# Banded attention with a two-layer network: the first block's second layer in another order of its tiles, with other landing times in the table that orders the work

## The chip, the cores and the metric

The kernel runs on one core of one Trainium2 chip. A core has five engines that each work through a list of instructions in order: PE (TensorE, matmuls into the PSUM banks), DVE (VectorE), ACT (ScalarE), POOL (GpSimd) and SP (SyncE). DMA transfers are issued from the lists of ACT, SP and POOL and are carried by 16 DMA engines. A transfer is recorded by a semaphore when it lands. The metric is the device time of one execution, in microseconds (us). Engines wait for each other through semaphores, and an instruction that waits holds everything behind it in its engine's list, DMA issues included.

## The reference

Attention over 8 batches, 8 heads, 576 positions and head size 64, in which a query sees itself and the 63 positions before it; then a two-layer network with a leaky activation over all 4608 tokens.

```python
scores = scale * np.matmul(q, k.transpose(0, 1, 3, 2))
mask = (rel >= 0) & (rel < window)                 # window = 64
attn = softmax(np.where(mask, scores, -1e9))
x = np.matmul(attn, v).transpose(0, 2, 1, 3).reshape(B * S, H * D)      # 4608 x 512
h = x @ w_in                                       # w_in 512 x 2048
g = np.maximum(0.01 * h, h)
return g @ w_out                                   # w_out 2048 x 512
```

The results are float32. The kernel gets that accuracy from matmuls on a shorter type by splitting each operand into a high and a low part and multiplying three times (high by high, high by low, low by high).

## The kernel before

**Stages.** The first three chunks of 512 tokens are done the plain way, while the weights are still unpacked. The other six chunks form three blocks (s = 0, 1, 2) of 1024 tokens, that is two half-tiles of 512 tokens, t = 0 and t = 1. The first layer of a block (line 1117, tiles `m{s}_{f}_{k}`) takes seven products instead of eight for each f of 0 to 7 (a Strassen scheme on sums of x and of w_in). The second layer of blocks 1 and 2 also goes in seven products (line 1180, tiles `z`), and needs sums of w_out; the second layer of block 0 goes the plain way (line 1137, tiles `y`): this is the loop at the end of the function, and I call it the y stage. In the trace it runs from about 427 to 544 us.

**The y stage.** Each half-tile t needs 16 row blocks f of g, taken in pairs. A pair p of column half j (f = 8j + 2p and the next) is 1024 wide. ACT makes its high part (`wide_high`, line 1162), DVE its low part (`wide_low`, line 1166), PE then does 24 matmuls into four PSUM banks, one bank for each 128 rows of the output. High and low parts have two buffers that take turns (`gs` and `pxa`). At the end of a half-tile the four banks are copied out (`put_out`, line 1140; banks 0 and 2 by DVE, 1 and 3 by ACT) and sent to `outT`. The next half-tile, and after it block 1, begins with bank 0 again, so these two places are seams: PE can't go on before the bank is copied.

**What stands beside it.** While the blocks run, attention goes on in units m of 128 tokens (two 64-position windows): scores on PE (line 278), a mask on DVE (666), a copy on ACT (672), the maximum over partitions on POOL (681), a subtraction on DVE (688), exp on ACT (692), the sum on POOL (684), five transfers on SP that gather and spread the sums (two at 695, one at 716, two at 728), the values on PE (740), a product on DVE (752), and a transfer to `x_rows` (755). Units 20 to 27 become the x of block 1 (`x_build`: a fetch at 867, sums on DVE at 874, casts on ACT at 893 and DVE at 896). The eight sums of w_out (`prepare(1, f)`) pass one after the other through one buffer, `pspare`: two fetches from `w_second` (1027, issued by ACT), an addition and four smaller ones on DVE (1032, 1035), a cast on ACT (1038), a subtraction on DVE (1041), and two transfers to `w_sums` (1045, issued by ACT). The next sum's fetch may not start before both have landed. Loads of q and k for a unit (170) and of v (174) are issued by ACT as well. The weights for PE are fetched by POOL (1101).

**What sets the order.** Nothing is ordered by hand here. Every step is entered as an `op` with an engine, a duration `us`, the steps that it needs, a `rank` (the smaller goes first), a `lag` after those steps, and `land`, the time that a transfer is taken to need. `arrange()` plays these numbers through and writes each engine's list; it also counts eight lanes, so that a transfer of ACT or SP is not placed before the one eight transfers earlier has landed by its numbers. On the chip the same eight lanes are semaphores: an issue waits until the earlier transfer on its lane has really landed. `bulk` enters ACT's transfers, `load` those of SP. A number of the table never changes what is computed, only where an instruction stands.

Of the kernel before, what the change touches and what calls it, by code (L numbers as in the profile page):

```python
# [86 lines left out]
IN_PREP_AT = (0, 0, 0, 6, 7, 0, 6, 7)  # L87
OUT_PREP = 1.0
IN_SEVEN = (1, 2)
KT = DM // P  # L90
FT = DF // P
# [13 lines left out]
def band_attention_ffn(ctx: ExitStack, tc: tile.TileContext, qk, vW, vL, w_in, w_out, eye_mask, out, outT):  # L105
# [433 lines left out]

    def bulk(fn, *after, rank=1.0, land=6.5):  # L540
        return op("ACT", 0.5, fn, *after, rank=rank, lag=1.0, land=land)

# [228 lines left out]
    def attend(m, gate):  # L771
# [4 lines left out]
        if m > PAIRED + 1:  # L776
            o["k"] = bulk(partial(load_qk, m), before["S"], rank=0.2 + late)
        elif m > PAIRED:
            o["k"] = bulk(partial(load_k, m, nc.scalar), before["S"], rank=0.2 + late)
        if m > PAIRED:  # L780
            o["v"] = bulk(partial(load_v, m, nc.scalar), before["X1"], rank=0.3 + late)
        takes = [before["take"], two["take"]] if m == EARLY else []
# [69 lines left out]
    def x_build(s, n, xt_of, xt_free, x_free):  # L852

        urge, wait = ((0.2, 0.2), (1.4, 2.6), (0.6, 2.6))[s]
        m = (UPC * LEAD + 2 * UPC * s) // UNITS + 2 * n

        def raw():
            return xt_of()[0].rearrange("p (i q c) -> p i q c", i=2, q=4)

        def sums():  # L860
            return xt_of()[1].rearrange("p (k i c) -> p k i c", k=4, i=2)

        def part(q):
            return raw()[:, :, q] if q < 4 else sums()[:, q - 4]

        def fetch():
            nc.sync.dma_start(
                xt_of()[0].rearrange("p (i c) -> p i c", i=2), x_rows[m : m + 2].rearrange("i p c -> p i c")
            )

        got = [load(fetch, *at[m]["kept"], *at[m + 1]["kept"], *xt_free, rank=urge, land=6.5)]

        def sub(to, a, b):
            nc.vector.tensor_tensor(part(to), part(a), part(b), ALU.subtract)

        d = op("DVE", 0.5, partial(sub, 4, 0, 2), *got, rank=urge, lag=wait)
        d3 = op("DVE", 0.5, partial(sub, 6, 1, 0), *got, rank=urge, lag=wait)
        d2 = op("DVE", 0.5, partial(sub, 5, 1, 4), d, rank=urge)
        d4 = op("DVE", 0.5, partial(sub, 7, 3, 5), d2, rank=urge)
# [12 lines left out]
        for a, b, after in ((0, 2, got), (2, 3, got), (3, 7, [d, d2, d3, d4])):  # L892
            hi = op("ACT", 0.2 + 0.213 * (b - a), lambda a=a, b=b: nc.scalar.copy(x_view(0, a, b), source(a, b)), *after, *x_free, rank=urge, lag=wait)
# [4 lines left out]
            done.append(op("DVE", 0.2 + 0.35 * (b - a), low, hi, rank=urge))  # L898
        return done
# [112 lines left out]
    def prepare(n, f, at, hurry, *freed):  # L1012
# [38 lines left out]
        written = [y for x in (f, f + half) for y in stores[x]] if n else []  # L1051
        got = [bulk(partial(fetch, i), *freed, *all_in, *written, rank=hurry + 0.1, land=6.5) for i in range(2)]
        if n:
# [6 lines left out]
        lo = op("DVE", 1.4, low, hi, rank=hurry)  # L1060
        prepared[n, f] = [bulk(partial(keep, i), lo, rank=hurry + 0.1, land=6.5) for i in range(2)]

# [140 lines left out]
    def second_in_seven(s):  # L1203
        WIDE, HIGH = 1.27, 1.07
        last_pair = at[NU // 2 - 1]
# [6 lines left out]
        for k, (slot, t, j) in enumerate(FACTORS):  # L1212
            b = bank_at(s, BANK_OF[k])
            for p in range(4):
# [20 lines left out]
                if p % 2 == 0:  # L1235
                    made_before = [y for f in range(half) for y in prepared[1, f]] if isinstance(slot, int) else []
                    q, got = filled(factor(slot, 2 * p), *made_before)
# [49 lines left out]
    for s in range(NS):  # L1287
# [42 lines left out]
        for t in range(2):  # L1330
            for f in range(FT):
                if f % 2 == 0:
                    q = next(pair_of)
                    j, p = f // half, f % half // 2
                    free = pair_free.get(q % 2, []) + (shut if q % 2 else [])
                    hi = op("ACT", 1.07, partial(wide_high, s, 2 * (q % 2), t, j, p), made[t, f], made[t, f + 1], *free, rank=0.2)
                    lo = op("DVE", 1.6, partial(wide_low, s, 2 * (q % 2), t, j, p), hi, rank=0.2)
                    split_of[t, f] = split_of[t, f + 1] = lo
                g_free[t, f] = [split_of[t, f]]
                if f % 2 == 0:  # L1340
                    n, got = filled(w_second[:, f : f + 2])
# [85 lines left out]
```

## Time and profile before

| what | value |
|---|---|
| three runs | 865.08, 867.63, 868.66 us (median 867.63) |
| profiled execution, its own time | 867.03 us |
| span of its records | 865.2 us |
| PE busy | 848.2 us, 98% |
| DVE, ACT, POOL busy | 72%, 44%, 43% |
| DMA from HBM and to it | 172.52 MB and 53.06 MB |
| y stage in the trace | about 427 to 544 us |

PE is busy nearly all the time, so the time of the kernel is PE's work plus the few places where PE stands still or runs at a lower clock. What ends a standstill is read in the view of waits and then in the timeline of the engine that is named there.

### The profile page before, as it was taken

Reading aid. Unit: us, or ns where it says so; the run is one execution under the profiler, and the core shown is the slowest. Engines: PE = TensorE matmul, PEld = TensorE weight load, DVE = VectorE, ACT = ScalarE, POOL = GpSimd, SP = SyncE. Lnnn points to the kernel's source line nnn. Section 1 sums busy time; section 2 is a strip of 40 time slices with the busy share of each in tenths; the row PEclk is TensorE's granted clock in tenths of the full one; section 3 lists DMA queues with packets and bytes.
Section 4 is the critical chain, followed back from the end, with each engine's and each line's share of the span. In section 5 each row is a group of like instructions: output and inputs, shape, how many; then the busy total and the mean of one; then the engine's idle time right before and its main releaser. Section 6 shows DMA issues by size and latency. Waiting matters only on the chain.

```text
span 865.2 us, 16790 instructions
## 1 busy us (share of the span) xinstructions
PE 848.2 (98%) x6778; PEld 688.3 (80%) x6778; DVE 623.6 (72%) x883; ACT 376.8 (44%) x605; POOL 368.0 (43%) x218
## 2 busy tenths in 40 slices
PE   9999999999999999999999899899999999999998
PEld 6787888888888888888887687688888888888886
DVE  7999885667788778665677879396579865536863
ACT  4665554334334353543533533244354433334431
POOL 5322000878888524667785757655110100011010
PEclk9999999999999999999999999899999999999999
DMA  9874856798899878899989997979987876666672
GB/s 328 259 247 132 267 170 239 249 299 274 295 315 331 274 241 281 299 314 355 305 291 351 306 367 238 373 233 331 284 236 228 235 245 221 193 183 189 204 210 92
DMA packets 99341, 226.80 MB, mean 262 GB/s; under 512 B 15552, under 2 KB 46400, under 8 KB 89792
## 3 DMA queue, kind: packets, MB, share of 16 engines
q0 software_dynamic: 23136, 90.18, 33.2%
q10 hardware_dynamic: 35664, 77.31, 27.0%
q1 hardware_dynamic: 40464, 58.24, 20.2%
q8 instruction: 53, 0.87, 0.4%
q14 instruction: 24, 0.20, 0.1%
HBM read 172.52 MB, written 53.06 MB: 261 GB/s over the span
## 4 chain that ended last, share of the span: by engine, by line
PE 81%; DMA 7%; DVE 6%; issue 2%; POOL 2%; ACT 1%; ACTq 0%; SPq 0%; POOLq 0%; DVEq 0%
PE m L1117 26%; PE z L1180 18%; PE acc L928 10%; PE h L919 10%; PE h L431 5%; PE acc L467 4%; PE s L278 3%; DMA rows<-late_c 3%; PE o L740 3%; DMA late_r<-rows 2%; POOL late_o L684 1%; DMA w_sums<-pspare 1%; DMA raw<-w_out 1%; PE o L367 1%; DVE pspare L1035 1%
## 5 line engine op out<-in xcount | busy, mean ns | idle before, releaser
L1117 PE MATMUL m<-pfew,p 128*128 128x512 f32 x720 | 170.7, 393 | 0.0
L1117 PEld LDWEIGHTS m<-pfew,p 128*128 128x128 f32 x720 | 135.5, 189 | 28.7
L928 PE MATMUL acc<-p,gs 128*128 128x512 f32 x324 | 80.6, 394 | 0.0
L1126 DVE TENSOR_TENSOR p<-m,pxa 128x512 f32<-128x512 f32 x60 | 41.4, 690 | 50.8 <-PE m L1117 50.5
L1101 POOL DMA_DIRECT2D p<-w_first x42 | 22.7, 541 | 124.4 <-PE m L1117 76.7
L1117 PE MATMUL m<-pxb,p 128*128 128x512 f32 x288 | 71.7, 396 | 3.7 <-ACT p L1129 3.7
L681 POOL PARTITION_ALL_REDUCE g<-late_f x20 | 38.7, 1966 | 83.8 <-DVE late_f L666 71.3
L684 POOL PARTITION_ALL_REDUCE late_o<-late_f x20 | 65.2, 3272 | 15.4 <-ACT late_f L692 8.6
L1129 ACT ACTIVATE p<-p 128x512 f32<-128x512 f32 x60 | 37.8, 631 | 76.7 <-DVE p L1126 71.8
L928 PEld LDWEIGHTS acc<-p,gs 128*128 128x128 f32 x324 | 59.8, 188 | 12.8
L1126 DVE TENSOR_TENSOR pxa<-m,pxa 128x512 f32<-128x512 f32 x60 | 41.3, 689 | 36.6 <-PE m L1117 35.8
L1117 PEld LDWEIGHTS m<-pxb,p 128*128 128x128 f32 x288 | 54.5, 191 | 15.6 <-ACT p L1129 4.1
L684 POOL PARTITION_ALL_REDUCE late_o<-e x18 | 59.9, 3347 | 13.2 <-ACT e L692 8.5
L684 POOL PARTITION_ALL_REDUCE late_o<-late_e x18 | 59.8, 3345 | 5.7 <-ACT late_e L692 5.4
L1180 PE MATMUL z<-gs,p 128*128 128x512 f32 x240 | 57.7, 389 | 0.0
L919 PE MATMUL h<-pxa,p 128*128 128x512 f32 x228 | 54.9, 390 | 0.0
L1180 PEld LDWEIGHTS z<-gs,p 128*128 128x128 f32 x240 | 45.1, 188 | 9.3
L1180 PE MATMUL z<-third,p 128*128 128x512 f32 x216 | 51.9, 389 | 0.0
L1180 PE MATMUL z<-pxa,p 128*128 128x512 f32 x216 | 51.9, 389 | 0.0
L1137 PE MATMUL y<-gs,p 128*128 128x512 f32 x192 | 47.4, 399 | 4.3 <-ACT pxa L1162 2.8
L919 PEld LDWEIGHTS h<-pxa,p 128*128 128x128 f32 x228 | 42.7, 188 | 9.0
L1137 PE MATMUL y<-pxa,p 128*128 128x512 f32 x192 | 47.3, 395 | 1.8 <-DVE pxa L1166 1.8
(191 smaller groups left out, 1715.8 us busy)
## 6 DMA issues: line engine op xcount, KB each, us to landing
p<-w_first POOLq DMA_DIRECT2D x42, 1024.0 KB, 6.1
p<-w_second POOLq DMA_DIRECT2D x28, 1024.0 KB, 6.7
p<-w_sums POOLq DMA_DIRECT2D x16, 1024.0 KB, 5.5
qk<-qk ACTq DMA_DIRECT2D x26, 512.0 KB, 6.0
pspare<-w_second ACTq DMA_DIRECT2D x16, 512.0 KB, 7.0
w_sums<-pspare ACTq DMA_DIRECT2D x16, 512.0 KB, 8.3
raw<-w_out ACTq DMA_DIRECT2D x15, 512.0 KB, 4.0
raw<-w_in ACTq DMA_DIRECT2D x14, 512.0 KB, 3.9
```

The source lines that it names most:

```text
L278: nc.tensor.matmul(ps[j][t, c : c + QB], k[i][s, p], q[s, w, p], start=not begun and (not more or (w, p) == (0, 0)), stop=not begun and no ...
L431: nc.tensor.matmul(ps, a[:, k, :], b[:, k, part], start=n == 0, stop=n == len(terms) - 1)
L467: nc.tensor.matmul(acc[c, i], a[:, ts], b, start=begin and n == 0, stop=end and n == 2)
L681: nc.gpsimd.partition_all_reduce(most_of(j), e_of(m)[:, j], P, ReduceOp.max)
L684: nc.gpsimd.partition_all_reduce(sum_of(j), e_of(m)[:, j], P, ReduceOp.add)
L919: nc.tensor.matmul(ps, a[:, k, :], b[:, k], start=i == 0, stop=i == len(terms) - 1)
L928: nc.tensor.matmul(acc[c, i], a[:, i * P : (i + 1) * P], b, start=begin and k == 0, stop=n in ends and k == 2)
L1117: nc.tensor.matmul(tiles[b], w[:, 256 * i + 128 * kt : 256 * i + 128 * kt + 128], x_part(OF_X[k], j, kt), start=begin and c == 0, stop=c = ...
L1126: nc.vector.tensor_tensor(to(), tiles[b], x(), ALU.add)
L1129: nc.scalar.activation(to(), to() if b is None else tiles[b], AF.Prelu, alpha=0.01)
L1137: nc.tensor.matmul(tiles[i], a, b, start=f == 0 and k == 0, stop=f == FT - 1 and k == 2)
L1180: nc.tensor.matmul(tiles[b + i], a, x, start=begin and f == 0 and c == 0, stop=f == half - 1 and c == 2, skip_group_check=not begin,)
```

## The change

In the y stage the pairs are taken tile by tile of g: for each p both column halves, (p, j = 0) and (p, j = 1), then the next p; before, all four p of the first half came first. A tile of g holds both halves of a pair, so it is done with after two neighbouring pairs. The four output rows of a half-tile are now staged in the tile of p = 3. The pair's high part is entered ahead of its weights' fetch, as before; only the position in the loop changes. The rest of the diff changes numbers of the table: the rank of the w_out sums (1.0 to 0.6), longer landings and lags for the loads of q, k and v of the units from 20 on, for the fetches and stores of the w_out sums and for the fetches of x, some durations, and the w_sums fetch for four f waits for those four sums instead of all eight.

```diff
-OUT_PREP = 1.0
+OUT_PREP = 0.6
-    def bulk(fn, *after, rank=1.0, land=6.5):
-        return op("ACT", 0.5, fn, *after, rank=rank, lag=1.0, land=land)
+    def bulk(fn, *after, rank=1.0, lag=1.0, land=6.5):
+        return op("ACT", 0.5, fn, *after, rank=rank, lag=lag, land=land)
-            o["k"] = bulk(partial(load_qk, m), before["S"], rank=0.2 + late)
+            o["k"] = bulk(partial(load_qk, m), before["S"], rank=0.2 + late, lag=1.0 + 2 * late, land=6.5 + 2 * late)
...
-            o["v"] = bulk(partial(load_v, m, nc.scalar), before["X1"], rank=0.3 + late)
+            o["v"] = bulk(partial(load_v, m, nc.scalar), before["X1"], rank=0.3 + late, lag=1.0 + 2 * late, land=6.5 + 2 * late)
...
-        got = [load(fetch, *at[m]["kept"], *at[m + 1]["kept"], *xt_free, rank=urge, land=6.5)]
+        got = [load(fetch, *at[m]["kept"], *at[m + 1]["kept"], *xt_free, rank=urge, land=8.0 if s else 6.5)]
...
-        got = [bulk(partial(fetch, i), *freed, *all_in, *written, rank=hurry + 0.1, land=6.5) for i in range(2)]
+        got = [bulk(partial(fetch, i), *freed, *all_in, *written, rank=hurry + 0.1, lag=1.0 + 2 * n, land=6.5 + 1.5 * n) for i in range(2)]
...
-        prepared[n, f] = [bulk(partial(keep, i), lo, rank=hurry + 0.1, land=6.5) for i in range(2)]
+        prepared[n, f] = [bulk(partial(keep, i), lo, rank=hurry + 0.1, land=6.5 + 3 * n) for i in range(2)]
...
-                    made_before = [y for f in range(half) for y in prepared[1, f]] if isinstance(slot, int) else []
+                    made_before = [y for f in range(2 * p, 2 * p + 4) for y in prepared[1, f]] if isinstance(slot, int) else []
...
-            for f in range(FT):
+            for f in (j * half + 2 * p + a for p in range(4) for j in range(2) for a in range(2)):
...
-                        where = t, 12 + i
+                        where = t, (6, 7, 14, 15)[i]
```

`late` is 0.45 for the units from 20 on and 0 before, so their loads of q, k and v go from lag 1.0 and landing 6.5 to 1.9 and 7.4. With n = 1 (the w_out sums) the fetches go from lag 1.0 and landing 6.5 to 3.0 and 8.0, and the stores from 6.5 to 9.5. The numbers of SP's small transfers stay. The durations entered for DVE's work on x in block 2 go from 0.5 to 0.42 a step, and those of the wide casts by a few hundredths. In the changed program the lines from 855 on are numbered one higher.

The first place is DVE's list at the seam between the half-tiles. `y_0_0` and `y_0_2` are banks 0 and 2 of half-tile 0, `pspare` is the buffer of a w_out sum, `gs` and `pxa` the low parts of a pair. Before:

```order
L688 TENSOR_TENSOR late_f<-s_0_4978,g 128x512
L1166 TENSOR_TENSOR gs_82<-p_33_3673,gs_81 128x1024
L688 TENSOR_TENSOR late_f<-s_1_4979,g 128x512
L1032 TENSOR_TENSOR pspare_1786<-pspare_1786 128x1024
L1140 COPY p_25_3089<-y_0_0_4619 128x512
L1140 COPY p_24_2972<-y_0_2_4631 128x512
```

With the change:

```order
L688 TENSOR_TENSOR late_f<-s_0_4997,g 128x512
L1167 TENSOR_TENSOR gs_82<-p_33_3674,gs_81 128x1024
L688 TENSOR_TENSOR late_f<-s_1_4998,g 128x512
L1141 COPY p_24_2972<-y_0_0_4620 128x512
L1141 COPY p_24_2972<-y_0_2_4636 128x512
```

The wide addition of a w_out sum no longer stands ahead of the copy of bank 0; it now comes two pairs later.

The second place is ACT's list at the seam between block 0 and block 1. `y_1_1` and `y_1_3` are banks 1 and 3 of half-tile 1, `m_0_0` is the first bank of block 1, which the second product group of block 1 needs again. Before:

```order
L1140 COPY p_26_3246<-y_1_1_5114 128x512
L672 COPY e<-s_0_5599 128x512
L672 COPY e<-s_1_5600 128x512
L1140 COPY p_23_2922<-y_1_3_5167 128x512
L170 DMA qk_83<-qk 128x1024
L1123 COPY pxa_39_5678<-m_0_0_5659 128x512
L1027 DMA pspare_1786<-w_second 128x2x512
L692 ACTIVATE e<-e 128x512
L1027 DMA pspare_1786<-w_second 128x2x512
L692 ACTIVATE e<-e 128x512
L1129 ACTIVATE p_33_3673<-p_33_3673 128x512
L1129 ACTIVATE p_36_3803<-m_0_0_5659 128x512
```

With the change:

```order
L1046 DMA w_sums<-pspare_1786 512x1x256
L1141 COPY p_23_2922<-y_1_1_5118 128x512
L1046 DMA w_sums<-pspare_1786 512x1x256
L692 ACTIVATE late_f<-late_f 128x512
L1141 COPY p_23_2922<-y_1_3_5135 128x512
L699 ACTIVATE late_c_1772<-late_c_1772 128x8
L1124 COPY pxa_39_5615<-m_0_0_5592 128x512
L692 ACTIVATE late_f<-late_f 128x512
L1130 ACTIVATE p_33_3674<-p_33_3674 128x512
L672 COPY e<-s_0_5638 128x512
L1130 ACTIVATE p_36_3805<-m_0_0_5592 128x512
L170 DMA qk_83<-qk 128x1024
```

The two halves of the next sum's fetch and the load of q and k stood ahead of the activation that frees the first bank of block 1 (the last row, `m_0_0` into `p_36`). With the change that activation stands ahead of the load of q and k, and the fetch comes nine rows behind the rows shown. One of a sum's two stores now stands between the copies of banks 1 and 3; before, both stood directly ahead of these rows.

The third place is ACT's list within the y stage, from the stores of one sum to the fetch of the next. `pxb` and `pfew` are casts of x for block 1. Before:

```order
L1045 DMA w_sums<-pspare_1786 512x1x256 x2
L672 COPY late_e<-s_0_4827 128x512
L170 DMA qk_84<-qk 128x1024
L672 COPY late_e<-s_1_4828 128x512
L692 ACTIVATE late_e<-late_e 128x512
L893 CAST pxb_3413<-p_36_3803 128x2x256
L1162 CAST gs_81<-p_25_3089 128x1024
L692 ACTIVATE late_e<-late_e 128x512
L174 DMA more_v<-vL 128x1024
L699 ACTIVATE late_c_1772<-late_c_1772 128x8
L893 CAST pfew_3422<-p_36_3803 128x256
L1027 DMA pspare_1786<-w_second 128x2x512 x2
```

With the change:

```order
L1046 DMA w_sums<-pspare_1786 512x1x256 x2
L894 CAST pfew_3420<-p_37_4012 128x256
L699 ACTIVATE late_c_1772<-late_c_1772 128x8
L1163 CAST gs_81<-p_24_2972 128x1024
L692 ACTIVATE late_e<-late_e 128x512 x2
L174 DMA more_v<-vL 128x1024
L1163 CAST pxa_38_4632<-p_24_2972 128x1024
L894 CAST pfew_3420<-p_37_4012 128x4x256
L672 COPY late_f<-s_0_4997 128x512
L672 COPY late_f<-s_1_4998 128x512
L170 DMA qk_83<-qk 128x1024
L1028 DMA pspare_1786<-w_second 128x2x512
```

Between the stores and the fetch one wide cast (1162) stood before, two stand now (1163). The load of q and k stood between two score copies; now it and the fetch stand directly ahead of a wide cast, which is the next row behind those shown. At two further places of the y stage the load of q and k stands now with only a sum's cast (1039) between it and a wide cast.

More of the change, by code (lines that the diff above doesn't have):

```diff
@@ L776, in attend @@
         if m > PAIRED + 1:
-            o["k"] = bulk(partial(load_qk, m), before["S"], rank=0.2 + late)
+            o["k"] = bulk(partial(load_qk, m), before["S"], rank=0.2 + late, lag=1.0 + 2 * late, land=6.5 + 2 * late)
         elif m > PAIRED:
-            o["k"] = bulk(partial(load_k, m, nc.scalar), before["S"], rank=0.2 + late)
+            o["k"] = bulk(partial(load_k, m, nc.scalar), before["S"], rank=0.2 + late, lag=1.0 + 2 * late, land=6.5 + 2 * late)
         if m > PAIRED:
-            o["v"] = bulk(partial(load_v, m, nc.scalar), before["X1"], rank=0.3 + late)
+            o["v"] = bulk(partial(load_v, m, nc.scalar), before["X1"], rank=0.3 + late, lag=1.0 + 2 * late, land=6.5 + 2 * late)
         takes = [before["take"], two["take"]] if m == EARLY else []
@@ L852, in x_build @@
     def x_build(s, n, xt_of, xt_free, x_free):
+        STEP, WIDTH = (0.42, 0.27) if s == 2 else (0.5, 0.35)
         urge, wait = ((0.2, 0.2), (1.4, 2.6), (0.6, 2.6))[s]
@@ L869, in fetch @@
             )
-        got = [load(fetch, *at[m]["kept"], *at[m + 1]["kept"], *xt_free, rank=urge, land=6.5)]
+        got = [load(fetch, *at[m]["kept"], *at[m + 1]["kept"], *xt_free, rank=urge, land=8.0 if s else 6.5)]
         def sub(to, a, b):
             nc.vector.tensor_tensor(part(to), part(a), part(b), ALU.subtract)
[L876 to L879, printed above, removed]
+        d = op("DVE", STEP, partial(sub, 4, 0, 2), *got, rank=urge, lag=wait)
+        d3 = op("DVE", STEP, partial(sub, 6, 1, 0), *got, rank=urge, lag=wait)
+        d2 = op("DVE", STEP, partial(sub, 5, 1, 4), d, rank=urge)
+        d4 = op("DVE", STEP, partial(sub, 7, 3, 5), d2, rank=urge)
         def x_view(i, a, b):
@@ L896, in low @@
                 nc.vector.tensor_tensor(x_view(1, a, b), source(a, b), x_view(0, a, b).bitcast(F32), ALU.subtract)
-            done.append(op("DVE", 0.2 + 0.35 * (b - a), low, hi, rank=urge))
+            done.append(op("DVE", STEP - 0.27 + WIDTH * (b - a), low, hi, rank=urge))
         return done
@@ L1203, in second_in_seven @@
     def second_in_seven(s):
-        WIDE, HIGH = 1.27, 1.07
+        WIDE, HIGH = 1.22, 1.06
         last_pair = at[NU // 2 - 1]
@@ L1335, in band_attention_ffn @@
                     free = pair_free.get(q % 2, []) + (shut if q % 2 else [])
-                    hi = op("ACT", 1.07, partial(wide_high, s, 2 * (q % 2), t, j, p), made[t, f], made[t, f + 1], *free, rank=0.2)
+                    hi = op("ACT", 1.06, partial(wide_high, s, 2 * (q % 2), t, j, p), made[t, f], made[t, f + 1], *free, rank=0.2)
                     lo = op("DVE", 1.6, partial(wide_low, s, 2 * (q % 2), t, j, p), hi, rank=0.2)
                     split_of[t, f] = split_of[t, f + 1] = lo
+                    n, got = filled(w_second[:, f : f + 2])
                 g_free[t, f] = [split_of[t, f]]
-                if f % 2 == 0:
-                    n, got = filled(w_second[:, f : f + 2])
                 for i in range(4):
```

## The prediction

> **What bounds the kernel now.** I read the head of the page first, then PE's waits.
>
> ```profile
> span 865.2 us, 16790 instructions
> PE 848.2 (98%) x6778; PEld 688.3 (80%) x6778; DVE 623.6 (72%) x883; ACT 376.8 (44%) x605; POOL 368.0 (43%) x218
> ```
>
> ```profile
> PE m L1117 <- ACT p L1129: 3.7, 1, 3.7
> PE y L1137 <- ACT pxa L1162: 2.8, 1, 2.8
> PE y L1137 <- DVE pxa L1166: 1.8, 2, 1.0
> PE y L1137 <- DVE gs L1166: 1.5, 1, 1.5
> ```
>
> PE's work sets the end, and the change takes none of it away. What can be won is PE's standstills. These five waits hold 9.8 us, and all lie in the y stage or just behind it; the list's other waits are smaller and lie in the first 70 us, where nothing changes. The windows of 10 us add that a long standstill costs more than itself (after the times: busy time of PE, PEld, DVE, ACT and POOL, then the granted clock):
>
> ```profile
> 460.00:470.00 10.00, 8.52 (x37) 6.74 (x38) 5.22 (x8) 4.04 (x8) 6.70 (x4) 1.00 1.01 357
> 480.00:490.00 10.00, 7.22 (x71) 5.33 (x72) 9.40 (x11) 5.14 (x9) 8.61 (x4) 0.86 1.01 325
> 550.00:560.00 10.00, 6.35 (x22) 4.86 (x21) 1.58 (x3) 3.43 (x8) 6.35 (x3) 0.77 1.06 376
> ```
>
> The wait of 1.5 left the clock at 1.00; those of 2.8 and 3.7 brought it to 0.86 and 0.77. Undisturbed, PE's pace is in the chain of waits, where 336 matmuls in a row take 76.16, that is 0.227 each, or 5.44 for a pair of 24:
>
> ```profile
> 632.96 76.16 PE z L1180 x336
> ```
>
> What the slow clock costs is in PE's timeline (start, duration, count; what counts is the distance from one start to the next):
>
> ```profile
> 470.76 0.27 PE L278 MATMUL s<-qk,qk 64*64 64x64 f32 x2
> 471.86 4.42 PE L1137 MATMUL y<-gs,p 128*128 128x512 f32 x18
> ...
> 485.80 3.01 PE L1137 MATMUL y<-gs,p 128*128 128x512 f32 x9 [2.78 <-ACT pxa L1162]
> 488.75 0.37 PE L278 MATMUL s<-qk,qk 64*64 64x64 f32 x2
> ...
> 490.65 3.03 PE L1137 MATMUL y<-gs,p 128*128 128x512 f32 x12
> ...
> 557.00 2.93 PE L1117 MATMUL m<-pxb,p 128*128 128x512 f32 x6 [3.65 <-ACT p L1129]
> 559.73 4.08 PE L1117 MATMUL m<-pfew,p 128*128 128x512 f32 x12
> 563.74 0.27 PE L278 MATMUL s<-qk,qk 64*64 64x64 f32 x2
> ```
>
> A unit's scores take 471.86 - 470.76 = 1.10 undisturbed. After the 2.78, nine matmuls took 2.95 (2.04 is due) and the scores 1.90: 1.71 lost. After the 3.65, six took 2.73 (1.36 due) and twelve 4.01 (2.72 due): 2.66 lost. So the seam between the half-tiles costs 2.78 + 1.71 = 4.49, the seam to block 1 costs 3.65 + 2.66 = 6.31, and the three waits within the stage 1.5 + 1.8 = 3.3 by the list above: **14.1 us in all**, the most that there is to win.
>
> The Trainium skill (TensorE: Matmul & The Clock Gate, Part 1, "What's actually happening") has the clock halved only after an idle window of about 3.4 us, in a window that runs freely. By that rule the 2.78 would have cost nothing beyond itself, and the gain below would be 1.7 smaller. The rows contradict it for this stall, and the sum goes by the rows.
>
> Next, why PE waited. ACT's timeline (ACTq rows are DMA issues):
>
> ```profile
> 462.15 0.33 ACTq L170 DMA_DIRECT2D qk<-qk  x1
> 462.58 0.59 ACT L672 COPY late_e<-s 128x512 f32<-128x512 f32 x1 [5.10 <-DMA rows<-late_c]
> 464.11 1.05 ACT L1162 CAST gs<-p 128x1024 fp32r<-128x1024 f32 x1
> ...
> 512.35 1.05 ACT L893 CAST pfew<-p 128x1024 fp32r<-128x1024 f32 x1 [4.66 <-DMA w_sums<-pspare]
> ...
> 545.45 0.59 ACT L1123 COPY pxa<-m 128x512 f32<-128x512 f32 x1 [1.02 <-PE m L1117]
> 552.21 0.57 ACTq L1027 DMA_DIRECT2D pspare<-w_second  x1
> 554.70 0.57 ACTq L1027 DMA_DIRECT2D pspare<-w_second  x1
> 556.37 0.58 ACT L1129 ACTIVATE p<-m 128x512 f32<-128x512 f32 x1
> ```
>
> ACT did nothing from 546.0 to 552.2, because the next row of its list was a fetch for a sum whose buffer was still being stored; the activation that frees block 1's first bank stood behind both halves of that fetch, and PE resumed as it ended (556.95). The waits of 5.10 and 4.66 are of the same kind: a load of q and k held until an earlier transfer on its lane had landed, and the second half of a sum's fetch, both with wide casts behind them. The waits of 1.5 and 0.8 within the stage follow these two; the one of 1.0 follows a low part that DVE began late. The landings in 440 to 560 us say why (median us from issue to landing last):
>
> ```profile
> w_sums<-pspare ACTq DMA_DIRECT2D x6, 512.0 KB, 11.7
> qk<-qk ACTq DMA_DIRECT2D x7, 512.0 KB, 8.0
> p<-x_rows SPq DMA_DIRECT2D x4, 512.0 KB, 9.6
> rows<-late_c SPq DMA_DIRECT2D x8, 4.0 KB, 6.7
> ```
>
> The table counted on 6.5 for the first three and 5.0 for the last. The seam between the half-tiles is another matter, for which DVE's and POOL's timelines are needed:
>
> ```profile
> 468.14 1.21 DVE L1166 TENSOR_TENSOR gs<-p,gs 128x1024 fp32r<-128x1024 f32 x1
> ...
> 481.84 0.68 DVE L688 TENSOR_TENSOR late_f<-s,g 128x512 f32<-128x512 f32 x1
> 482.44 2.66 DVE L1032 TENSOR_TENSOR pspare<-pspare 128x1024 f32<-128x1024 f32 x1
> 485.02 1.27 DVE L1140 COPY p<-y 128x512 f32<-128x512 f32 x2
> ...
> 528.93 1.21 DVE L1032 TENSOR_TENSOR pspare<-pspare 128x1024 f32<-128x1024 f32 x1
> ```
>
> ```profile
> 481.49 3.52 POOL L684 PARTITION_ALL_REDUCE late_o<-late_f  x1
> ```
>
> The view of waits names ACT, but its cast had ended by 485.1. Bank 0 was copied by DVE from 485.02 (half of 1.27 for the first of two), and PE went on at 485.80. Ahead of that copy stood the wide addition of a w_out sum, which took 2.66 beside a POOL sum and 1.21 without one.
>
> **The change part by part.** The sum is made against the profiled execution's own 867.03 (span 865.2); the median of the runs, 867.63, is 0.60 above it.
>
> *Fetch and q, k load behind the activation at the seam to block 1.* The activation that frees the first bank waits no longer for a landing ahead of it, except through the two stores, which wait for a lane. PE needs the first bank only after a group of seven products, 42 x 0.227 = 9.5 after the seam. I take the whole 6.31. The lower end: if a store is held as long as the longest hold above, the 6.2 before 552.21, while the copy of bank 3 behind it is due after three products (18 x 0.227 = 4.1), then 2.1 and a slow clock of 1.7 come back, and the gain is 2.5.
>
> *Addition away from the seam between the half-tiles.* Without it the copy of bank 0 starts when the row ahead ends, at 482.52 instead of 485.02, and the first copy, half of 1.27, ends at 483.2; PE had stopped at 485.80 - 2.78 = 483.02. So 0.2 of the 4.49 stays: +4.3. The row ahead (688) still waits for POOL; if POOL is 2.5 late there, all of it is back: from 0 to 4.3, and I take 4.3, since that wait is 0 in the row above.
>
> *Longer landings and lags elsewhere.* The new numbers (9.5 for stores, 7.4 for q and k, 8.0 for x) lie between the old ones and those measured. With two wide casts instead of one between a sum's stores and the next fetch there are two pairs, at least 10.9, for a landing of 11.7. For SP's small transfers the table keeps 5.0 against 6.7, so lanes still come free late. I take half of the 3.3: +1.6, from 0 to 3.3.
>
> *New standstills.* Every list from the end of the early part on is dealt anew, and the trace doesn't show the new neighbours. The bounds: none, and one stall as dear as the dearest in the trace, 6.3. I take the middle: -3.2.
>
> *Tile by tile.* PE's matmuls and their number stay. The sums of x for block 1 may start two to three pairs earlier, because a tile of g is finished after two pairs; the last x, however, waits for unit 27 and stays where it was. Nothing waits for x but block 1, and no such wait is in the list: 0. Staging all output rows in the tile of p = 3 costs 0 as long as block 1 writes that tile only with f = 6, six groups or 57 us after the seam.
>
> *Last w_out sum.* Its stores move from behind the first copy of group 6 of block 1 to behind that of group 7, about 9.5 later:
>
> ```profile
> 624.84 0.59 ACT L1123 COPY pxa<-m 128x512 f32<-128x512 f32 x1
> DMA to landing us min/median/max: 3.3/8.3/14.8
> p<-w_sums POOLq DMA_DIRECT2D x16, 1024.0 KB, 5.5
> ```
>
> The copy of group 7 is the first row; the second is for line 1045. Stores at about 626 land by 641 at the latest; the second half of the first z product that needs the sums begins 72 matmuls into z, at 632.96 + 16.3 = 649.3, and its fetch needs 5.5. That leaves 2.8: 0, and one for one if it is used up.
>
> Sum: 6.31 + 4.3 + 1.6 - 3.2 = 9.0 off 867.03 gives 858.0; the median to expect is **858.6**.
>
> **The rivals.** *The sum's work moves to the seam to block 1.* In DVE's new list the whole of a w_out sum stands between the last low part of the block and the copy of bank 0. The four smaller additions and the subtraction cover 1024 columns each time, as the wide addition does, so the sum takes three times 1.21 to 2.66, and the two masks between take about 0.68 each, as line 688 does for the same shape: 5.0 to 9.3, of which I take the middle, 7.2. If the low part is only just in time, the pair takes 23 x 0.227 = 5.2 more, so 7.2 + 0.6 - 5.2 = 2.6 and a slow clock of 1.7 come back: 858.6 + 4.3 = 862.9. Against it: two pairs of PE work stand there, if DVE is ahead. The Trainium skill (SBUF — State Buffer, "Who interferes with whom") says that a DVE instruction with two inputs in SBUF is blocked by a POOL instruction that reads SBUF; the 2.66 against 1.21 agrees, and it speaks for this rival.
>
> *The holds stay, only elsewhere.* The bytes are the same, and the DMA share is at 1.0 in the rows of 460 to 490. If landings grow as issues bunch, as many waits appear as go: 867.
>
> *Slower: q and k loads directly ahead of wide casts.* Three of them now stand with a sum's cast or fetch, or nothing, between them and a wide cast. A pair leaves 5.44 - 1.05 - 1.21 = 3.2 of play for a held ACT. A hold of h costs h - 3.2 + 1.7. At 6.0 that is 4.5 each and 13.5 for three, 4.5 more than the forecast gain: 872. It decides from a mean hold of about 6.0. For it: holds of 5.1 and 6.2 did occur, and landings of sums reach 14.8. Against: the loads are entered later after the scores, and a table that expects later landings spaces the lanes wider.
>
> *The change doesn't do what it says:* sums placed later. In DVE's list the three sums of the y stage do stand two pairs later; this is not a case by itself.
>
> **How the numbers follow.** Forecast 0.58; sum at the next seam 0.15; holds stay 0.14; slower 0.13. What a measurement of this kernel can tell from no change is about 0.5%, 4.3 us. Of the forecast's share 0.04 falls short of that bound; of the first rival (4.7 off the median) half counts on each side. Faster 0.58 - 0.04 + 0.07 = 0.61; same 0.04 + 0.08 + 0.14 = 0.26; slower 0.13. The forecast's own range is 854 to 863: all of the 14.1 won gives 853.5, and new standstills of 6.3 with nothing won inside the stage give 863. The range for all cases is 852.5 (the floor, less a microsecond of spread) to 870, which leaves out most of the slower case and little else.
>
> **What would show it.** In the new trace PE's waits on L1130 at block 1's start and on the first row of `y_1` are gone or under 1; the granted clock is 1.00 from 440 to 600; between two wide casts no ACT idle time over 3.2 ends with a DMA. Wrong it would be if PE's waits in 330 to 640 sum to more than 7, if the copy of bank 0 at the seam to block 1 begins late, or if ACT's longest holds (now 6.2) precede wide casts.

## The result, and the profile after

The changed kernel takes **852.71 us** in the median of six runs (850.80 to 856.05); the kernel before took 867.24 in the same comparison (864.91 to 868.66). The ratio is 0.9841, with a 95% interval of 0.9814 to 0.9867. The change is faster by 14.5 us, where the forecast was 9.0 and a median of 858.6.

The profiled execution is the longest of the six, 856.05 us. The head of its page and the first rows of PE's waits:

```profile
span 854.3 us, 16788 instructions
PE 843.8 (99%) x6778; PEld 687.5 (80%) x6778; DVE 617.4 (72%) x883; ACT 375.5 (44%) x605; POOL 366.3 (43%) x218
```

```profile
PE y L1138 <- DVE gs L1167: 3.7, 1, 3.7
PE idle L503 <- DVE p L514: 1.4, 1, 1.4
```

All five waits quoted of before are gone, and one new one of 3.7 has come; the 1.4 is in the first 70 us and was there before. The chain of waits shows what that is worth in time: the first `z` product (632.96 before) starts 10.98 earlier, and everything behind it takes as long as before.

```profile
621.98 76.16 PE z L1181 x336
```

The windows of 10 us (busy time of PE, PEld, DVE, ACT, POOL, granted clock, DMA share) show both seams whole, and the clock down in one place only, behind the new wait:

```profile
480.00:490.00 10.00, 10.00 (x132) 8.22 (x131) 9.93 (x13) 3.67 (x6) 5.93 (x4) 1.00 1.06 400
520.00:530.00 10.00, 8.14 (x114) 6.56 (x115) 8.28 (x11) 2.44 (x4) 5.37 (x3) 0.83 0.77 235
550.00:560.00 10.00, 10.00 (x104) 8.17 (x103) 5.89 (x10) 4.87 (x9) 7.36 (x4) 1.00 1.04 357
```

At the seam between the half-tiles DVE's timeline (start, duration) has the copy of bank 0 directly behind line 688, 6 us earlier than the 485.02 of before, and PE goes on without a wait:

```profile
478.45 0.68 DVE L688 TENSOR_TENSOR late_f<-s,g 128x512 f32<-128x512 f32 x1
479.06 1.27 DVE L1141 COPY p<-y 128x512 f32<-128x512 f32 x2
```

At the seam to block 1 ACT's timeline has the activation that frees the first bank 8.3 us after the first product of block 1 (536.65; before 543.64 and 12.7). The fetch of the next sum comes later than it did, 14.4 after that product instead of 8.6, but PE no longer waits behind it:

```profile
544.98 0.60 ACT L1130 ACTIVATE p<-m 128x512 f32<-128x512 f32 x1 [0.21 <-PE m L1118]
546.15 0.34 ACTq L170 DMA_DIRECT2D qk<-qk  x1
551.09 1.24 ACTq L1028 DMA_DIRECT2D pspare<-w_second  x2
```

The new wait, in the timelines of DVE and of PE:

```profile
512.70 0.68 DVE L688 TENSOR_TENSOR late_e<-s,g 128x512 f32<-128x512 f32 x1
519.22 0.69 DVE L752 TENSOR_TENSOR late_n<-o,late_r 128x512 f32<-128x512 f32 x1 [5.84 <-issue]
519.83 1.98 DVE L1167 TENSOR_TENSOR gs<-p,gs 128x1024 fp32r<-128x1024 f32 x1
```

```profile
517.79 0.39 PE L1138 MATMUL y<-gs,p 128*128 128x512 f32 x1
521.86 5.07 PE L1138 MATMUL y<-gs,p 128*128 128x512 f32 x14 [3.68 <-DVE gs L1167]
526.86 0.27 PE L278 MATMUL s<-qk,qk 64*64 64x64 f32 x2
```

DVE stood for 5.84 us ahead of the product of line 752, with the wide low part of pair 14 behind it. The profile names no transfer for this wait, but the product needs the spread sums, `late_r`. Of their two transfers, issued at 508.06 and 509.51, the first landed 10.1 us after its issue, where the table has 5.0; the landing of the second isn't recorded.

**The account.** The view of waits counts from the modelled end of a matmul. What a stall really costs is read from one start to the next, with 0.227 for each matmul and 1.10 for the scores of a unit taken off:

| place | matmuls, start to start | lost (us) | wait listed |
|---|---|---|---|
| before, pair 6 | 6, 467.54 to 470.76 | 1.86 | 1.5 |
| before, seam between half-tiles | 45 and scores, 477.28 to 493.61 | 5.03 | 2.8 |
| before, pair 13 | 15, 519.92 to 524.51 | 1.19 | 0.8 |
| before, pair 15 | 21, 534.52 to 540.66 | 1.38 | 1.0 |
| before, seam to block 1 | 24, 551.83 to 563.74 | 6.47 | 3.7 |
| after, pair 14 | 15, 517.79 to 526.86 | 5.67 | 3.7 |

Before lost 15.9, the changed kernel 5.7 in this execution; the difference, 10.3, and 0.4 that it gained ahead of the y stage make 10.7 of the 10.98. Its fastest run took 850.80, and 867.03 - 15.9 - 0.4 is 850.7. That run has no trace, so it is by its time alone that nothing of the five stalls is left in it and nothing new has come. The stalls are those of one execution of each kernel; another execution of the lists of before, shown below, has them in other sizes.

### The profile page after: what moved, and what is told of

It is laid out like the page before. It is cut to its first block, busy times and chain, and to the rows that moved or that the text cites. A ratio compares the mean times of both kernels' runs of the same rounds, so it can differ in the third digit from the quotient of the medians.

```text
span 854.3 us, 16788 instructions
## 1 busy us (share of the span) xinstructions
PE 843.8 (99%) x6778; PEld 687.5 (80%) x6778; DVE 617.4 (72%) x883; ACT 375.5 (44%) x605; POOL 366.3 (43%) x218
## 4 chain that ended last, share of the span: by engine, by line
PE 92%; DMA 5%; DVE 2%; SPq 1%; ACT 0%; issue 0%; ACTq 0%; DVEq 0%
PE m L1118 27%; PE z L1181 18%; PE acc L929 11%; PE h L920 10%; PE y L1138 7%; PE h L431 5%; PE acc L467 5%; PE s L278 4%; PE o L740 3%; DMA x_rows<-late_n 1%; DMA rows<-late_c 1%; DMA late_c<-late_o 1%; PE o L367 1%; DMA raw<-w_out 1%; SPq L728 0%; PE t L393 0%
## 5 line engine op out<-in xcount | busy, mean ns | idle before, releaser
L684 POOL PARTITION_ALL_REDUCE late_o<-late_f x20 | 65.9, 3317 | 12.3 <-ACT late_f L692 8.2
L681 POOL PARTITION_ALL_REDUCE g<-late_f x20 | 36.4, 1855 | 79.3 <-DVE late_f L666 71.3
L1102 POOL DMA_DIRECT2D p<-w_second x28 | 19.4, 691 | 73.0 <-PE z L1181 35.3
```

The source lines that it names most:

```text
L681: nc.gpsimd.partition_all_reduce(most_of(j), e_of(m)[:, j], P, ReduceOp.max)
L684: nc.gpsimd.partition_all_reduce(sum_of(j), e_of(m)[:, j], P, ReduceOp.add)
L1102: nc.gpsimd.dma_start(to, of)
```

## The experiments

Three readings (the expectations call them theories) had to be told apart. **A**: each standstill belongs to one row that stands in the wrong place. **C**: the new order of the pairs is the gain. **D**: transfers land later than the table says because the DMA engines are full, an engine that issues them is held, and where that hits PE changes with the list and from one execution to the next. Each kernel was timed against the one before, on the same chip as the others of its group (median of before: 866.44 where a single row of it was moved, for the order of the pairs alone and for everything else alone; 866.59 for the two groups of numbers, the row of the new standstill and the change again; 866.84 for both rows moved, less traffic and SP's small transfers).

**One row moved at the seam between the half-tiles.** In the kernel before, the finished list is taken and the addition of line 1032 that stands directly ahead of the copy of bank 0 is put behind that of bank 2 (`behind(x, y)` takes x out and puts it behind y):

```diff
-    for x in arrange():
+    order = arrange()
...
+    vector = [x for x in order if x["engine"] == "DVE"]
+    k = next(i for i, x in enumerate(vector) if x is copies[0, 0])
...
+    behind(vector[k - 1], copies[0, 2])
...
+    for x in order:
```

> The kernel before with one row moved: in DVE's list at the seam between the half-tiles, the wide addition of a w_out sum (line 1032) goes behind the two copies of banks 0 and 2. Theory A (the row in front of the bank's copy sets the stall): the stall of 2.78 us and the slow clock behind it go, 4.5 to 5.0 us faster (about 862.5 beside 867.2), and PE's wait on the first row of y_1 is under 0.5. Rival (the wait belongs to ACT's cast, which the view of waits names): no change, and the wait stays at 2 to 3 us.

Measured: 858.20, ratio 0.9917 (0.9886 to 0.9947), 8 us faster, where theory A had 4.5 to 5.0. PE's timeline and ACT's:

```profile
481.07 2.32 PE L1140 MATMUL y<-gs,p 128*128 128x512 f32 x9 [0.24 <-ACT late_f L692]
497.13 7.14 PE L1140 MATMUL y<-gs,p 128*128 128x512 f32 x23 [2.05 <-DVE gs L1169]
538.97 0.40 PE L1120 MATMUL m<-pxb,p 128*128 128x512 f32 x1
```

```profile
544.62 0.57 ACTq L1028 DMA_DIRECT2D pspare<-w_second  x1
547.04 0.58 ACT L1132 ACTIVATE p<-m 128x512 f32<-128x512 f32 x1
```

The wait at the seam is 0.24 instead of 2.78: the addition was its cause, and not the cast of ACT that the view of waits named. But a new wait of 2.05 came on pair 10, the waits on pairs 13 and 15 went, that on pair 6 went although the lists up to it are those of before, and the seam to block 1 has no wait although both halves of the fetch still stand ahead of its activation. They were issued 5.7 us after the first product of block 1, where it was 8.6 before. So the places are not independent, which reading A alone has no account of.

**One row moved at the seam to block 1.** In the same way, on ACT, both halves of line 1027 that stand ahead of the activation of `m_0_0` go behind it:

```diff
+    ahead = [x for x in scalar[k - 8 : k] if any(x is y for z in fetches.values() for y in z)]
...
+    for x in ahead[::-1]:
+        behind(x, freeing[1, 0])
```

> The kernel before with the two halves of one fetch for a w_out sum moved, in ACT's list, from ahead of the activation that frees the first bank of block 1 to behind it. Theory A: the stall of 3.65 us at block 1's start and its slow clock go, 6.3 to 6.5 us faster (about 861). Rival (a store that waits for a lane, or the copy of bank 3, then holds ACT just as long): 0 to 2.5 us faster.

Measured: 865.76, ratio 0.9994 (0.9970 to 1.0017): no difference, against theory A, and not by the way that its rival named (a store or a copy that holds ACT). The stall is gone from its place; the activation ends 7.6 us after the first product (543.38). It is paid back 10 and 21 us later, in the timelines of ACT, DVE and PE:

```profile
550.41 0.60 ACT L1132 ACTIVATE p<-m 128x512 f32<-128x512 f32 x1
553.36 2.34 ACTq L1028 DMA_DIRECT2D pspare<-w_second  x2
```

```profile
561.98 1.23 DVE L1033 TENSOR_TENSOR pspare<-pspare 128x1024 f32<-128x1024 f32 x1 [1.93 <-DMA pspare<-w_second]
572.10 0.68 DVE L1129 TENSOR_TENSOR pxa<-m,pxa 128x512 f32<-128x512 f32 x1
572.70 3.46 DVE L1172 TENSOR_TENSOR p<-p 128x1024 f32<-128x1024 f32 x1
576.08 1.48 DVE L1129 TENSOR_TENSOR pxa<-m,pxa 128x512 f32<-128x512 f32 x2
```

```profile
564.46 3.02 PE L1120 MATMUL m<-pxb,p 128*128 128x512 f32 x12 [0.81 <-DVE p L1129]
576.81 2.50 PE L1120 MATMUL m<-pfew,p 128*128 128x512 f32 x6 [2.70 <-DVE pxa L1129]
579.11 3.69 PE L1120 MATMUL m<-pxb,p 128*128 128x512 f32 x12
```

The fetch is issued no earlier than before (553.36; before 552.21) and lands later (median of its two halves 7.0 us after the issue; before 5.4). PE no longer stands while it lands, so the sum's additions, a wide addition of 3.46 and with them the sums that free PE's banks (line 1129) fall later in PE's program: 0.8 and 2.7 of waiting, and about 1.8 more at a lower clock (the next 18 matmuls took 5.83, from 576.81 to 582.64, and 4.08 is due). That is 5.3 of the 6.5. In the change the list of DVE has the wide additions of the second layer (560.31 and 561.57) ahead of the sum's (564.97, after 1.57 of waiting for the fetch), and PE doesn't wait there.

Up to the seam to block 1 the lists of this kernel are those of before, so its trace is a second execution of that part (pair 6, then the seam between the half-tiles):

```profile
470.68 1.82 PE L1140 MATMUL y<-gs,p 128*128 128x512 f32 x5 [3.46 <-DVE gs L1169]
487.07 2.29 PE L1140 MATMUL y<-gs,p 128*128 128x512 f32 x9 [1.32 <-ACT p L1143]
```

Pair 6 waits 3.46, where it was 1.48, and the seam 1.32, where it was 2.78, although the addition again takes 2.66 ahead of the copy: PE came there later. The same lists lose time at the same places, but not the same amounts.

**Both rows moved.**

> The kernel before with both rows moved (the addition behind the copies of banks 0 and 2, the fetch behind the activation). If each gain stands by itself: 8.2 + 0.7 = 8.9 us faster than before, about 857.5. If the seam to block 1 is already free once the first seam is (the single move of the addition left no wait there), the second move adds nothing or costs: 858 to 861.

Measured: 862.16, ratio 0.9948 (0.9930 to 0.9965). Each against its own before, that is 4.7 us won, where the addition alone won 8.2 (the two intervals overlap a little). The expectations, 857.5 if each gain stands by itself and 858 to 861 if not, were both too low. The gains don't add. In the traces, from the first product of block 1 to the first `z` product it takes 87.9 us (541.66 to 629.56), with the addition alone 83.5 (538.97 to 622.51): the moved fetch costs 4.4, again as a wait of 2.7 on line 1129. And the seam between the half-tiles stands again, by another way (ACT, DVE, PE):

```profile
478.93 1.08 ACT L672 COPY late_f<-s 128x512 f32<-128x512 f32 x2 [7.43 <-DMA pspare<-w_second]
481.43 0.69 DVE L688 TENSOR_TENSOR late_f<-s,g 128x512 f32<-128x512 f32 x1 [6.64 <-POOL g L681]
485.22 3.49 PE L1140 MATMUL y<-gs,p 128*128 128x512 f32 x9 [3.46 <-ACT late_f L692]
```

ACT was held for 7.43 us at a load of q and k; the score copies behind it were late, POOL's maximum after them, line 688, and the copy of bank 0 behind 688. Up to this place the lists are those of the first experiment, where it was 0.24.

**The order of the pairs alone, and everything else alone.** First the kernel before with only the two lines on the loop and the staging tile, then the changed kernel with these two undone:

```diff
-            for f in range(FT):
+            for f in (j * half + 2 * p + a for p in range(4) for j in range(2) for a in range(2)):
...
-                        where = t, 12 + i
+                        where = t, (6, 7, 14, 15)[i]
```

> The kernel before with the new order of the pairs alone, all numbers of the table as before. In its lists the wide addition stands one wide low part further ahead of the copy of bank 0, and no fetch stands ahead of the activation that frees block 1's first bank. Theory A (only the rows at the two seams count): 9 to 11 us faster, 856 to 858. Theory B (the longer landings are what keeps ACT free): holds come back at other rows, and it is within 4 us of before.

> The changed kernel with the old order of the pairs, half by half; all its new numbers stay. At its seams the addition is away from the copy of bank 0 and the fetch is behind the activation, while a load of q, k and one of v stand ahead of that activation. Theory A: 9 to 14 us faster than before, 853 to 858, near the change itself. Theory B says the same. Theory C (the new order is the gain: x for block 1 is ready earlier, tiles come free earlier): within 4 us of before.

Measured: 860.87, ratio 0.9941 (0.9921 to 0.9962), for the order alone; 854.15, ratio 0.9868 (0.9834 to 0.9902), for the numbers alone. The order alone wins 5.6, less than theory A's 9 to 11 and more than theory B's 4 at most. In its lists the addition stands a few rows further ahead of the copy, and no fetch stands ahead of the activation, but a load of v does (issued at 552.01). There are waits again, at pair 6, at the seam between the half-tiles and in block 1:

```profile
471.12 2.79 PE L1137 MATMUL y<-gs,p 128*128 128x512 f32 x11 [2.44 <-DVE gs L1166]
487.03 5.94 PE L1137 MATMUL y<-gs,p 128*128 128x512 f32 x18 [2.30 <-ACT p L1140]
553.77 1.65 PE L1117 MATMUL m<-pxb,p 128*128 128x512 f32 x6 [1.34 <-ACT p L1129]
```

The numbers alone win 12.3, and their interval overlaps that of the whole change: reading C is out, and what the order adds beside them can't be measured. This kernel also settles the first rival of the prediction, since its DVE list holds a whole w_out sum ahead of the copy of bank 0 at the seam to block 1:

```profile
523.69 1.21 DVE L1033 TENSOR_TENSOR pspare<-pspare 128x1024 f32<-128x1024 f32 x1
531.13 0.68 DVE L1141 COPY p<-y 128x512 f32<-128x512 f32 x1
```

```profile
PE m L1118 <- DVE p L1141: 0.3, 1, 0.3
```

The sum was done early, and PE waited 0.3 (the second fence is from the view of waits). In the change itself DVE, done with the same sum, waited 3.19 us for PE ahead of that copy, which began at 534.81.

**The two groups of numbers apart.** The kernel before with only the numbers of the w_out sums (`OUT_PREP`, `prepare`, `made_before`), and with only `lag=1.0 + 2 * late, land=6.5 + 2 * late` at the loads of q, k and v:

> The kernel before with only the new numbers of the w_out sums: rank 0.6, the longer lags and landings of their fetches and stores, and the w_sums fetch that waits for four sums. Order of the pairs and the loads' numbers as before. In its lists no addition stands at the seam between the half-tiles, no fetch stands ahead of the activation of m_0_0, but a load of q, k and one of v do, and one sum's addition and four smaller ones stand ahead of the copy of bank 0 at the seam to block 1. Theory S (a w_out sum that runs later than its table is what stops PE at both seams and, behind them, in block 1): 8 to 12 us faster than before, 854 to 858. Rival L (the loads of q, k, v hold ACT just as much): under 5 us faster.

> The kernel before with only the new lags and landings of the loads of q, k and v from unit 20 on. The wide addition still stands directly ahead of the copy of bank 0 at the seam between the half-tiles, and half a fetch with a load of q, k ahead of the activation of m_0_0. Theory S: 0 to 3 us faster. Rival L: 6 us or more.

Measured: 856.05, ratio 0.9872 (0.9851 to 0.9893), and 858.23, ratio 0.9900 (0.9878 to 0.9923). The first is as theory S said, the second is against it: the loads' numbers win 8.4 by themselves, as rival L had it, and the addition is still directly ahead of the copy of bank 0 (DVE's timeline of the second kernel, and its waits):

```profile
480.43 1.21 DVE L1032 TENSOR_TENSOR pspare<-pspare 128x1024 f32<-128x1024 f32 x1
481.56 0.68 DVE L1140 COPY p<-y 128x512 f32<-128x512 f32 x1
```

```profile
PE y L1137 <- ACT p L1140: 1.1, 1, 1.1
```

No POOL sum lies beside the addition here, and a POOL maximum begins only after it (480.69). It takes 1.21, not 2.66, and the copy comes 3.5 us earlier than before. Each group alone wins most of what both win; 10.5 and 8.4 don't add up to 12.3. The first leaves waits of 1.8 and 2.2 close behind each other (pairs 11 and 12), the second one of 3.1 (pair 14).

**Less traffic.** The kernel before and the changed one with their lists unchanged; each fetch of w_out in the y stage leaves out the second half of its bytes, so part of the result is computed on other data:

```diff
+    def fill_half(n, of):
...
+        nc.gpsimd.dma_start(to[:, :1], of[:, :1])
...
-                    n, got = filled(w_second[:, f : f + 2])
+                    n, got = filled(w_second[:, f : f + 2], fill=fill_half)
```

> The kernel before with its lists unchanged and less traffic: each fetch of w_out for a pair of the y stage brings only its first 512 KB instead of 1024 KB (the second half of the tile keeps what stood there, so half of the second layer of block 0 is computed on other data; matmuls and their number stay). That takes some 5.6 MB of the 37.8 MB between 440 and 560 us away. Theory D (PE stands still because transfers land later than the table says, and they land late because the DMA engines are full): the landing of the sums' stores falls from 11.7 to 9 us or less, and the kernel is 6 to 13 us faster, 854 to 861. Rival (the standstills are fixed by the order of the lists, whatever the landing): within 3 us of before.

> The changed kernel with the same reduced fetches (half of the second layer of block 0 is computed on other data). Theory D: the differences between its executions, which come from late landings, go, and all lie between 850 and 852.5, the floor that PE's work sets. Rival: median and spread as for the change, 853 and some 5 us.

Measured: 857.12, ratio 0.9901 (0.9877 to 0.9924), and 850.55, ratio 0.9819 (0.9795 to 0.9843), five runs of it from 849.95 to 851.80. Both as theory D said, though the second isn't shown to be faster than the change itself, whose interval in its second comparison (0.9821 to 0.9879, below) overlaps with it. From 440 to 560 us the lighter kernel before moved 34.23 MB, the kernel before 37.81. The landings of the lighter kernel before (440 to 560 us; KB each, median us from issue to landing), where 11.7, 8.0, 9.6 and 6.7 stood:

```profile
w_sums<-pspare ACTq DMA_DIRECT2D x6, 512.0 KB, 8.6
qk<-qk ACTq DMA_DIRECT2D x8, 512.0 KB, 6.6
p<-x_rows SPq DMA_DIRECT2D x4, 512.0 KB, 6.1
rows<-late_c SPq DMA_DIRECT2D x7, 4.0 KB, 5.2
```

With the lists unchanged, the waits on pairs 13 and 15 and at the seam to block 1 are gone. What is left in the stage is 0.89 on pair 6 (1.48 before) and the seam between the half-tiles, whose addition is fixed in the list and lies beside POOL (DVE, then PE):

```profile
481.31 2.66 DVE L1032 TENSOR_TENSOR pspare<-pspare 128x1024 f32<-128x1024 f32 x1
483.89 1.28 DVE L1145 COPY p<-y 128x512 f32<-128x512 f32 x2
484.67 2.32 PE L1142 MATMUL y<-gs,p 128*128 128x512 f32 x9 [2.48 <-ACT pxa L1167]
```

So reading D holds for the seam to block 1 and the waits on pairs 13 and 15, and reading A for this one place. That the engines are full is not all of it: the kernel with the numbers alone moved more in the same window (41.23 MB, at a share of 1.02), and the stores of its sums landed in 6.7 in the median. The Trainium skill (DMA: Bandwidth & Descriptors, "Latency and other measured facts") has the fixed cost of a transfer smaller when HBM is less loaded; the 4 KB transfer that went from 6.7 to 5.2 agrees with it. In the kernel with the numbers alone it took 5.6 at the full load, so the load isn't its only cause.

**The row of the new standstill moved, and the change again.** In the changed kernel the product of line 752 goes behind the wide low part of pair 14; beside it the changed kernel unaltered:

> The changed kernel with one row moved: on DVE the product of line 752 that waited 5.84 us in the profiled execution of the change goes behind the wide low part of pair 14 of the y stage. Theory P (that row is the new standstill, and it makes the slower executions of the change): the runs between 853 and 856 go, median 850.5 to 851.5, all within 2 us of each other. Rival (the late landing only moves its wait to the next row, as with the moved fetch): median and spread as for the change itself in this same comparison, within 1 us.

> The changed kernel once more, as the measure for the others of this comparison. If what differs from one execution to the next is how long transfers take to land, its executions spread over 850.5 to 856 again, and the profile shows a stall at another place or none; if the stall is fixed by the list, the profile shows it at pair 14 again, with 3 to 4 us.

Measured: 853.53 (850.64 to 854.74), ratio 0.9840 (0.9818 to 0.9862), and 853.01 (851.96 to 859.85), ratio 0.9850 (0.9821 to 0.9879). Theory P falls: the move is worth nothing that shows. In this execution of the unaltered change the wait on pair 14 isn't there; both kernels have the same smaller one, on pair 12:

```profile
506.85 0.73 PE L1138 MATMUL y<-gs,p 128*128 128x512 f32 x2 [1.41 <-DVE gs L1167]
```

The 5.7 of the first profile was one execution's, not the list's. Together with the lighter kernel, whose runs lie within 1.9 us of each other, this points to late landings as what makes the spread. It isn't shown: the eleven runs of the order of the pairs alone lie within 2.7 us at the full traffic, so the list has a part in it.

**SP's small transfers at their measured landing.** In the changed kernel `land=5.0` becomes `land=5.0 + 4 * late` for the transfers that gather and spread the sums:

> The changed kernel with the landing of SP's small transfers (the gathered and spread sums) in the table at 6.8 instead of 5.0 for the units from 20 on, near the 6.6 to 7.7 that the trace shows. Theory D: these were the last numbers too small, so the remaining waits shrink and the median is 850.5 to 852. Rival (a new list is a new draw): anything from 851 to 858, with waits at other pairs.

Measured: 852.03 (851.75 to 853.04), ratio 0.9837 (0.9814 to 0.9860). The trace shows no wait of PE between 425 us and the end, and the five runs lie closer together than those of the change. Its interval overlaps with theirs, so it isn't shown to be faster.

## Why the prediction was right or wrong

**Bound and direction: right.** PE's standstills were what could be won, and they were won: by its time, 15.9 of 15.9 in the best run. The time, 852.71, is 5.9 below the forecast, below the forecast's own range (854 to 863) and just inside the wide one (852.5 to 870). Of the 5.5 us between the forecast gain and the measured one, 2.8 is the term for the longer landings, 1.3 that for new standstills, 0.9 the two seams, and 0.4 was won ahead of the stage.

**"14.1 us in all": too small by 1.8.** The waits' view was added up for three of the stalls, and the two seams were counted only over the groups directly behind them. From start to start they are 15.9.

**Fetch and q, k load behind the activation, +6.31: the size was right, the reason was not enough.** The wait is gone and was worth 6.47. But the fetch moved alone won nothing, since the same late landing came out again 10 and 21 us later on line 1129. In the change the sum's work behind the fetch gives way too; that this is what makes it a gain there is read from the lists and wasn't tested by itself. My lower end of 2.5 looked for the cost in ACT's list; it lay in DVE's.

**Addition away from the first seam, +4.3: right, and worth 5.03.** The move alone took the wait from 2.78 to 0.24. In the second execution of the old lists the same place cost only 1.32, so the size is that of one execution. The bound I gave (all of it back if line 688 is 2.5 late) came true in the kernel with both rows moved.

**Longer landings, +1.6: the step that failed most.** Half of 3.3 was taken, because SP's numbers stayed too small. All of it was won, 4.4 from start to start; the loads' numbers alone move the kernel by 8.4. I counted late landings as a term beside the seams, where they are a cause that the seam to block 1 shares with the stage: with less traffic and the old list that seam is free. It was free with the addition moved too, so they are not the only one.

**New standstills, -3.2: near in size by luck, and of another kind.** The term was the middle of two bounds. 5.7 in the profiled execution, none in the best run, about 2 in the median (852.71 less 850.80). I took it for a property of the new list; it differs from one execution to the next of the same list.

**Tile by tile, 0: wrong alone, right beside the numbers.** It removes no work, but it deals the lists anew, and that alone was 5.6. With the new numbers nothing of it can be measured.

**Last w_out sum, 0: right.** No wait stands at the start of `z`.

**The rivals.** The whole sum ahead of a bank's copy does no harm where DVE is ahead (0.3). *The holds stay* is half right: ACT is still held 6.34 and 5.51 us in the profile of the change,

```profile
493.16 1.05 ACT L1039 CAST pspare<-pspare 128x1024 fp32r<-128x1024 f32 x1 [6.34 <-DMA x_rows<-late_n]
519.87 0.21 ACT L699 ACTIVATE late_c<-late_c 128x8 f32<-128x8 f32 x1 [5.51 <-DMA late_c<-late_o]
```

and the stores of the sums land hardly sooner than the 11.7 of before:

```profile
w_sums<-pspare ACTq DMA_DIRECT2D x6, 512.0 KB, 10.8
```

The first of these holds has a load of q and k with a sum's cast, and then a wide cast, behind it, as the slower rival had it at 6.0; PE did not wait, so its 3.2 of play was too little. The second lies beside the one wait that came, but not in its way: the high part of pair 14 had been cast at 512.78, and DVE held the low part. Of the signs named, the clock at 1.00 from 440 to 600 failed in that one window (0.83), an ACT idle time above 3.2 that ends with a DMA is still there, and one of ACT's longest holds does precede a wide cast; the waits of 330 to 640 sum to 3.7, under the 7 named.

**Still open** is why the lists of before were hit so hard. Five edits of it that have little in common (the addition moved, the order of the pairs, the sums' numbers, the loads' numbers, less traffic) each took 5.6 to 10.5 us away, and beyond the late landings no one cause was found that they share. A rival stands untested: the order and both groups of numbers also deal a new list, and perhaps most other lists would win as much. No table was run whose numbers were changed to no purpose, or made smaller.

## What to carry to other kernels

Where a table of expected times orders the work, compare its landings with the traced ones while the DMA engines are full: here, moving them towards those won 12.3, and no single row or order won more than 8.2. In both cases tried here a late transfer wasn't cured by moving the row that waits for it; follow what the landing releases, through every engine, to where PE meets it next. And price a stall from one start to the next, with the slow matmuls behind it, and look at a second execution before a single wait is called the list's.

## What the runs showed of the hardware

A gap's length alone doesn't tell whether the clock falls. After gaps of 2.05 and 2.30 the granted clock fell: 18 matmuls took 5.87 us (487.03 to the next scores at 492.90) where 4.08 is due, and the window's clock was 0.86. After 2.44 and 2.48 it stayed at 1.00 (2.30 and the first row are of the order of the pairs alone, 2.48 and the second row of the lighter kernel before):

```profile
480.00:490.00 10.00, 7.70 (x28) 5.97 (x27) 9.93 (x15) 5.98 (x11) 7.91 (x6) 0.86 0.92 278
480.00:490.00 10.00, 7.52 (x92) 5.78 (x91) 9.96 (x14) 5.08 (x10) 7.83 (x5) 1.00 0.82 261
```

The Trainium skill (TensorE: Matmul & The Clock Gate, Part 1, "What's actually happening") explains a varying onset by a window that runs freely, and that fits; its length of 3.4 us of idleness doesn't, since 2.05 was enough. A wide DVE addition with two inputs took 1.21 us alone (528.93 in the kernel before), 2.66 beside a POOL sum at the seam, and 3.46 at line 1172 in block 1, again beside a POOL sum (572.89 to 576.07). With both rows moved it took only 1.46 (at 485.64) beside a POOL sum that had begun at 483.50, so the size of the loss isn't settled by lying beside one.

The DMA share in the y stage doesn't tell how PE fares: it was 0.93 between 440 and 560 us in the kernel before with five waits, and 1.02 in the last experiment with none. That the time from issue to landing against the number in the table tells it better isn't shown either: in the last experiment the loads of q and k landed in 8.4, where the table has 7.4, and PE had no wait.
